# Linear attention with an ELU feature map on one core: three input buffers each instead of six, and a TensorE loop of three heads in nine turns

## The chip, the core and the metric

The kernel runs on one core of one Trainium2 chip. The metric is the device time of one execution in microseconds (us), median over the runs. Everything is bfloat16 in and out, with sums in fp32.

## What is computed

```python
B, H, S, D = 1, 32, 2048, 128
phi_q = where(q > 0, q + 1, exp(q)) + 1e-6
phi_k = where(k > 0, k + 1, exp(k)) + 1e-6
kv  = einsum("bhsd,bhse->bhde", phi_k, v)
z   = einsum("bhsd->bhd", phi_k)
num = einsum("bhqd,bhde->bhqe", phi_q, kv)
den = einsum("bhqd,bhd->bhq", phi_q, z)[..., None] + 1e-6
out = num / den
```

There are 32 independent heads. Each head reads q, k and v (512 KB each) and writes out (512 KB): 4 transfers of 512 KB a head, 128 in all.

## The kernel before, in words

A head's 2048 rows lie as 16 tiles of 128 x 128, 16 rows to a partition. The map phi(x) is formed as max(x, 0) + (min(exp(x), 1) + 1e-6). For a head h the steps are:

- **Loads** (L310 to L324): SyncE (SP) issues k, q and v into `k_sb`, `q_sb`, `v_sb`, each with `NBI` buffers (L189), head h in buffer h % NBI. Only v of head 0 has a buffer and a queue of its own (`v0_sb`, issued by ScalarE, L315).
- **k's map**: ScalarE forms exp(k) (`ek_sb`, L328), GpSimd max(k, 0) (`rk_sb`, L330), VectorE min(exp(k), 1) + 1e-6 (`emk_sb`, L334), and GpSimd adds the two for five of the sixteen tiles (L339). Both L328 and L330 read k's buffer.
- **kv and z**: TensorE multiplies phi(k)'s tiles with v into `kvz_ps` (L355, with one more column for z, L358), ScalarE and VectorE copy it out (L363, L365).
- **q's map**: TensorE transposes the 16 tiles of q into `x_ps` (L373), ScalarE, VectorE form exp, max and min from there (L384, L387, L390, L393).
- **Output**: TensorE multiplies phi(q) with kv into five banks `o_ps` (L411, L417), VectorE divides into `o_sb` (ten buffers, L432 and L438), and SP stores the head (L472).

**The order on each engine** is not the order of the text. A planner (`Plan`, L20) gets every step with a key, sorts each engine's steps by it (L54) and places a semaphore wait wherever a step reads or overwrites what another engine made. Keys are in heads. The keys of SP's queue matter here:

```python
load("k", k_sb, kf, h - NBI - (1.0 if h < 3 else 1.95))
load("v", v_sb, vf, h - NBI - 0.8)
load("q", q_sb, qf, h - NBI - 0.9)
late = h + 1.0 + 0.18 * h      # key of the store of head h
```

A load of head h waits until buffer h % NBI is free, that is, until the steps of head h - NBI that read it are done. SP works strictly in order: a load that waits holds up whatever stands behind it. The store's key grows by 1.18 a head and the load's by 1, so the stores fall back behind the loads in the queue as the kernel goes on; the last ten or so stores are issued after the last load.

**TensorE's program** has nine steps a head (two of transposes, two of kv, five output banks) after one step of warming up. It runs in three parts: some heads written out, then a hardware loop whose waits add a register to their constants, then the rest written out (`run`, L123). The loop begins at step 1 + LOOP * 9, has NBI * 9 steps and TURNS turns (L480): here 54 steps, or six heads, in four turns. L132 to L136 demand that the steps of all turns have the same waits and the same answer to whether the step raises a semaphore; a step raises one only where another engine needs it (`needed`).

Of the kernel before, what the change touches and what calls it, by code (L numbers as in the profile page):

```python
# [11 lines left out]
def _ap(base: bass.AP, elem_offset: int, dims):  # L12
    return bass.AP(base.tensor, base.offset + elem_offset, [list(base.ap[0])] + [list(d) for d in dims])
# [6 lines left out]
class Plan:  # L20
# [9 lines left out]
    def add(self, eng, key, emit, reads=(), writes=(), dma=None):  # L30
        op = Op()
        op.eng, op.key, op.emit, op.dma = eng, key, emit, dma
        op.deps, op.needed, op.clock = [], False, None
        op.reads, op.writes = tuple(reads), tuple(writes)
        for r in op.reads:
            w = self.writer.get(r)
            if w is not None:
                op.deps.append(w)
            if r[0].startswith("bank"):
                op.deps += [x for x in self.readers.get(r, []) if x.eng != eng]  # L40
        for r in op.writes:
            w = self.writer.get(r)
            if w is not None and (w.eng != eng or w.dma):
                op.deps.append(w)
            op.deps += [x for x in self.readers.get(r, []) if x.eng != eng or x.dma]
        for r in op.reads:
            self.readers.setdefault(r, []).append(op)
        for r in op.writes:
            self.writer[r] = op
            self.readers[r] = []  # L50
        self.ops.append(op)
        return op
# [7 lines left out]
    def emit(self, block, sems, dma_sem, loop):  # L60


        order = self.order()
        for op in self.ops:
            for d in op.deps:
                if not (d.eng == "pe" and op.eng == "pe"):
                    d.needed = True
        counts = {}
        for e, ops in order.items():
            n = 0  # L70
# [15 lines left out]
        while left:  # L86
            moved = False
            for e, ops in order.items():
                while at[e] < len(ops):
                    op = ops[at[e]]  # L90
# [85 lines left out]
def bass_standalone__linear_attn_elu__prompt_kernel(  # L176
# [9 lines left out]
    NH = B * H  # L186
    bf16 = mybir.dt.bfloat16
    fp32 = mybir.dt.float32
    NBI = 6  # L189
    NBO = 10  # L190
    NC = D + 1
    NB = 5
# [18 lines left out]

    PIECES = {NH - 2: ((0, 6), (6, NT)), NH - 1: ((0, 6), (6, 12), (12, NT))}
    EXTRA = {NH - 2: 0, NH - 1: 1}
    LOOP, TURNS = 3, 4

    qf = q.rearrange("b h s d -> (b h) s d")
    kf = k.rearrange("b h s d -> (b h) s d")
# [3 lines left out]
    with ExitStack() as es:  # L221
        def sb(name, shape, dt):
            return es.enter_context(nc.sbuf_tensor(name, shape, dt))

        k_sb = sb("k_sb", [P, NBI, NT * D], bf16)
        v_sb = sb("v_sb", [P, NBI, VW], bf16)
        q_sb = sb("q_sb", [P, NBI, NT * D], bf16)
        v0_sb = sb("v0_sb", [P, NT * D], bf16)
# [23 lines left out]

        for n, c in (("k", NBI), ("q", NBI), ("v", NBI), ("o", NBO + 3), ("x", 1)):
            for i in range(c):
# [17 lines left out]
        vfull = v_sb[:, :, :]  # L272
        pl.add("pool", -7, lambda g: g.memset(_ap(vfull, 0, [[VW, NBI], [GAP + GRP, 3], [1, GAP]]), 1.0), writes=[("vones",)])

# [31 lines left out]
        for h in range(NH):  # L306
            def at(name, key, h=h):
                return place.get((name, h), h + key)

            bi, b2, b3, bo = h % NBI, h % 2, h % 3, h % NBO  # L310

# [197 lines left out]
```

## Time and profile before

| | |
|---|---|
| median of 3 runs | 170.68 us (170.58 to 170.76) |
| the profiled execution's own time | 170.68 us |
| its span, first to last instruction | 168.8 us |
| TensorE's granted clock, mean | 0.994 |
| busy: PE / ACT / DVE / POOL | 158.0 / 157.3 / 149.6 / 105.5 us |
| moved by DMA | 67.31 MB, 399 GB/s over the span |

Outside the span lie 170.68 - 168.8 = 1.88 us. PE is TensorE's matmul, ACT ScalarE, DVE VectorE, POOL GpSimd, SP SyncE. The slices of the page are 168.8 / 40 = 4.22 us wide, a 9 in a row of slices means 90% or more. The DMA rows count packets on the core's 16 DMA engines; a transfer has landed when all 16 have marked it done.

### The profile page before, as it was taken

How to read it: one execution, taken by the hardware profiler on the slowest of the kernel's cores; microseconds unless marked ns; L12 is line 12 of the kernel's file. 1: busy time of each engine (PE TensorE's matmuls, PEld its weight loads, DVE VectorE, ACT ScalarE, POOL GpSimd, SP SyncE). 2: the span in 40 equal slices, each digit the busy share in tenths (PEclk: the TensorE clock that was granted, in tenths of full speed). 3: DMA queues.
4: the chain of work that ended last, by engine and by line, in shares of the span. 5: the costliest groups of instructions: out<-in, count | busy, mean ns of one | idle time of the engine just before them, and what ended most of it. 6: DMA issues, size and time to landing. Idle time of an engine off the chain costs nothing.

```text
span 168.8 us, 6570 instructions
## 1 busy us (share of the span) xinstructions
PE 158.0 (94%) x3089; PEld 151.7 (90%) x2401; DVE 149.6 (89%) x293; ACT 157.3 (93%) x180; POOL 105.5 (62%) x72
## 2 busy tenths in 40 slices
PE   7588999999999999999999999999999999999940
PEld 0488999999999999999999999999999999999830
DVE  0144999999999999999999999999999999999870
ACT  4599999999999999999999999999999999996960
POOL 3836866666677776666667776666667776666000
PEclk9999999999999999999999999999999999999997
DMA  5999999999999999999999999999999999999982
GB/s 204 412 414 411 412 406 409 406 415 408 411 414 409 415 416 415 418 413 419 415 414 415 416 413 420 413 419 415 413 416 418 417 414 415 411 413 415 412 333 104
DMA packets 22848, 67.31 MB, mean 399 GB/s; under 512 B 2097, under 2 KB 2609, under 8 KB 22833
## 3 DMA queue, kind: packets, MB, share of 16 engines
q1 hardware_dynamic: 22688, 66.59, 98.5%
q10 hardware_dynamic: 144, 0.52, 0.8%
q8 instruction: 9, 0.15, 0.3%
q14 instruction: 7, 0.05, 0.1%
HBM read 50.33 MB, written 16.78 MB: 398 GB/s over the span
## 4 chain that ended last, share of the span: by engine, by line
PE 87%; DMA 3%; DVE 3%; ACT 3%; issue 0%; SPq 0%
PE kvz_ps L355 36%; PE o_ps L411 32%; PE x_ps L373 16%; DMA q_sb<-in_q_dram 3%; DVE o_sb L438 1%; PE o_ps L277 1%; ACT eq_sb L384 1%; PE o_ps L417 1%; PE kvz_ps L277 1%; ACT ek_sb L328 1%; ACT rq_sb L387 1%; DVE emk_sb L334 0%; DVE rden_sb L460 0%; DVE den_sb L456 0%; SPq L320 0%
## 5 line engine op out<-in xcount | busy, mean ns | idle before, releaser
L384 ACT ACTIVATE eq_sb<-x_ps 128x1024 bf16<-128x1024 bf16 x64 | 72.4, 1349 | 3.4 <-PE x_ps L373 3.4
L339 POOL TENSOR_TENSOR rk_sb<-rk_sb,emk_sb 128x640 bf16<-128x640 bf16 x32 | 44.7, 1396 | 47.4 <-DVE emq_sb L393 41.2
L328 ACT ACTIVATE ek_sb<-k_sb 128x2048 bf16<-128x2048 bf16 x32 | 72.2, 2256 | 1.7 <-DMA k_sb<-in_k_dram 1.7
L438 DVE TENSOR_TENSOR o_sb<-o_ps,rden_sb 128x768 bf16<-128x768 f32 (+2 forms) x63 | 68.0, 1119 | 0.1
L355 PE MATMUL kvz_ps<-v_sb,rk_sb 128*128 128x128 bf16 (+1 forms) x512 | 67.6, 218 | 0.0
L330 POOL TENSOR_SCALAR rk_sb<-k_sb 128x2048 bf16<-128x2048 bf16 x32 | 60.6, 1892 | 2.7 <-DMA k_sb<-in_k_dram 2.0
L411 PE MATMUL o_ps<-kvs_sb,emq_sb 128*128 128x129 bf16 x474 | 60.6, 220 | 0.3 <-DVE o_sb L438 0.3
L411 PE MATMUL o_ps<-kvs_sb,rq_sb 128*128 128x129 bf16 x474 | 60.6, 220 | 0.0
L355 PE MATMUL kvz_ps<-v_sb,emk_sb 128*128 128x128 bf16 (+1 forms) x352 | 55.4, 219 | 1.2 <-DVE kvs_sb L365 1.2
L277 PE MATMUL kvz_ps<-ones_sb,rk_sb 128*128 128x1 bf16 x388 | 53.3, 166 | 0.0
L355 PEld LDWEIGHTS kvz_ps<-v_sb,rk_sb 128*128 128x128 bf16 x512 | 47.0, 97 | 1.5
L411 PEld LDWEIGHTS o_ps<-kvs_sb,rq_sb 128*128 128x128 bf16 x474 | 46.2, 97 | 0.0
L411 PEld LDWEIGHTS o_ps<-kvs_sb,emq_sb 128*128 128x128 bf16 x474 | 45.4, 97 | 0.6 <-DVE o_sb L438 0.4
L387 ACT ACTIVATE rq_sb<-x_ps 128x1024 bf16<-128x1024 bf16 x32 | 43.7, 1366 | 0.0
L277 PE MATMUL kvz_ps<-ones_sb,emk_sb 128*128 128x1 bf16 x228 | 37.8, 167 | 0.0
L373 PE MATMUL x_ps<-ident,q_sb 128*128 128x128 bf16 x512 | 34.6, 222 | 1.7 <-DMA q_sb<-in_q_dram 1.7
L373 PEld LDWEIGHTS x_ps<-ident,q_sb 128*128 128x128 bf16 x512 | 30.6, 99 | 5.6 <-DMA q_sb<-in_q_dram 5.6
L355 PEld LDWEIGHTS kvz_ps<-v_sb,emk_sb 128*128 128x128 bf16 x352 | 33.9, 97 | 1.5 <-issue 1.5
L334 DVE TENSOR_SCALAR emk_sb<-ek_sb 128x2048 bf16<-128x2048 bf16 x32 | 21.8, 682 | 8.8 <-ACT ek_sb L328 8.8
L390 DVE TENSOR_SCALAR rq_sb<-x_ps 128x1024 bf16<-128x1024 bf16 x32 | 21.8, 680 | 2.5 <-ACT eq_sb L384 2.5
L393 DVE TENSOR_SCALAR emq_sb<-eq_sb 128x2048 bf16<-128x2048 bf16 x32 | 22.1, 691 | 0.4 <-ACT eq_sb L384 0.4
L363 ACT ACTIVATE kvs_sb<-kvz_ps 128x128 bf16<-128x128 f32 x32 | 20.3, 634 | 0.0
(39 smaller groups left out, 78.2 us busy)
## 6 DMA issues: line engine op xcount, KB each, us to landing
k_sb<-in_k_dram SPq DMA_DIRECT2D x32, 512.0 KB, 13.2
q_sb<-in_q_dram SPq DMA_DIRECT2D x32, 512.0 KB, 13.2
v_sb<-in_v_dram SPq DMA_DIRECT2D x31, 512.0 KB, 13.6
out_dram<-o_sb SPq DMA_DIRECT2D x30, 512.0 KB, 13.8
out_dram<-o_sb SPq DMA_DIRECT2D x3, 192.0 KB, 4.7
v_sb<-in_v_dram ACTq DMA_DIRECT2D x1, 512.0 KB, 4.4
out_dram<-o_sb SPq DMA_DIRECT2D x1, 320.0 KB, 5.6
out_dram<-o_sb SPq DMA_DIRECT2D x1, 128.0 KB, 4.0
```

Source lines behind the costliest of these rows:

```text
L277: return pe.add_instruction(mybir.InstMatmult(name=nc.get_next_instruction_name(), engine=mybir.EngineType.PE, ldweights=False, ins=[pe.lo ...
L328: lambda a, bi=bi, b2=b2: a.activation(ek_sb[:, b2, :], k_sb[:, bi, :], ACT.Exp),
L330: pl.add("pool", h, lambda g, bi=bi, b3=b3: g.tensor_scalar(rk_sb[:, b3, :], k_sb[:, bi, :], BIG, 0.0, op0=ALU.min, op1=ALU.max), reads=[( ...
L334: lambda d, b2=b2, b3=b3: d.tensor_scalar(emk_sb[:, b3, :], ek_sb[:, b2, :], 1.0, EPS, op0=ALU.min, op1=ALU.add),
L339: pl.add("pool", h + 0.5, lambda g, added=added: g.tensor_tensor(out=added(rk_sb), in0=added(rk_sb), in1=added(emk_sb), op=ALU.add), reads ...
L355: last = pe.matmul(kvz_ps[:, 1 - l:NC + r], lhsT=w, rhs=rhs, start=first, stop=fin, skip_group_check=True)
L373: last = pe.transpose(xT_ps[:, j * P:(j + 1) * P], q_sb[:, bi, j * P:(j + 1) * P], ident[:])
L384: lambda a, b2=b2, c=cols(half): a.activation(eq_sb[:, b2, c], xT_ps[:, c], ACT.Exp),
L387: lambda a, b3=b3, c=cols(1): a.activation(rq_sb[:, b3, c], xT_ps[:, c], ACT.Relu),
L393: lambda d, b2=b2, b3=b3: d.tensor_scalar(emq_sb[:, b3, :], eq_sb[:, b2, :], 1.0, EPS, op0=ALU.min, op1=ALU.add),
L411: last = pe.matmul(o_ap, lhsT=x[:, b3, t * P:(t + 1) * P], rhs=kvs_sb[:, b3, :], start=first, stop=not first)
L438: return lambda d: d.tensor_tensor(out=o_sb[:, bo, t0:t1, :].rearrange("p (a b) d -> p a b d", b=n), in0=_ap(nfull(b), 512 * b + NC * (t0 ...
```

## The change

The number of buffers of k, q and v goes from six to three. The loop of TensorE's program follows it, since its size is NBI heads: 27 steps instead of 54, beginning at step 19 instead of 28, in nine turns instead of four. So 27 heads' worth of steps run in the loop where 24 did, and 8 heads' worth are written out in the program (2 before, 3 in the loop, 3 after) where 14 were (3, 6, 5). `Plan.emit` gets a passage that makes the answer of `needed` the same for a step in all turns: if one turn's step must raise its semaphore, those of all turns do.

```diff
@@ Plan.emit
+        eng, lo, size, turns = loop
+        for i in range(lo, lo + size):
+            turned = order[eng][i:lo + size * turns:size]
+            needed = any(op.needed for op in turned)
+            for op in turned:
+                op.needed = needed
@@ the kernel
-    NBI = 6
+    NBI = 3
     NBO = 10
@@
-    LOOP, TURNS = 3, 4
+    LOOP, TURNS = 2, 9
```

All keys that contain NBI move with it: the loads' keys become larger by 3, the stores' keys stay.

## The prediction

> **What bounds the kernel now.** I read the page's busy line first, then its slices, then the chain.
>
> ```profile
> PE 158.0 (94%) x3089; PEld 151.7 (90%) x2401; DVE 149.6 (89%) x293; ACT 157.3 (93%) x180; POOL 105.5 (62%) x72
> ...
> DMA  5999999999999999999999999999999999999982
> ...
> q8 instruction: 9, 0.15, 0.3%
> ...
> PE 87%; DMA 3%; DVE 3%; ACT 3%; issue 0%; SPq 0%
> ```
>
> Two resources are full at once. TensorE carries 87% of the chain; its timeline has the heads 4.73 us apart (kv of head 24 starts at 122.47, of head 30 at 150.86: 28.39 / 6) and no wait after 13.4 us. The DMA engines are full from the second slice to the 38th. Landing after landing, a transfer of 512 KB takes 1.27 us, so a head's four need 5.08 us, more than TensorE's 4.73. The stores' growing delay hides that: with 1 / 1.18 = 0.85 stores a head, 3.85 transfers need 4.89 us, still 0.16 too many. Loads therefore start with a lead and lose it. The next view is SP's: a load's time from issue to landing, over all of k.
>
> ```profile
> DMA to landing us min/median/max: 3.2/13.2/14.8
> ```
>
> The 3.2 is the first load, into an empty queue (1.27 of it data); 13.2 is ten transfers waiting ahead, not the memory being slow. The lead itself I take from the trace's landings beside the first instruction that reads the buffer: k of head 10 lands 7.1 us early, v of head 25 3.3, v of head 30 2.5. These are v of head 30's rows, SP's timeline and TensorE's:
>
> ```profile
> 134.87 0.55 SPq L320 DMA_DIRECT2D v_sb<-in_v_dram  x1
> ```
> ```profile
> DMA to landing us min/median/max: 13.5/13.5/13.5
> ```
> ```profile
> 150.86 0.22 PE L355 MATMUL kvz_ps<-v_sb,emk_sb 128*128 128x129 bf16 x1
> ```
>
> Issue 134.87 + 13.46 = 148.33 landed, 150.86 read: 2.5 us early. Last comes the end, in windows (DVE, ACT, PE busy; last two columns DMA share and GB/s):
>
> ```profile
> 162.00:164.00 2.00, 0.50 (x9) 0.33 (x6) 1.70 (x4) 1.68 (x6) 0.00 (x0) 1.00 0.86 337
> 164.00:166.00 2.00, 0.00 (x0) 0.00 (x0) 0.00 (x0) 0.00 (x0) 0.00 (x0) 1.00 0.68 253
> 166.00:168.80 2.80, 0.00 (x0) 0.00 (x0) 0.00 (x0) 0.00 (x0) 0.00 (x0) 0.66 0.06 24
> ```
>
> Compute is over at 164. The last store is issued at 164.38 and lands at 168.34. Of its 16 marks the first comes 1.74 us after the issue, the last 3.96: one DMA engine is 2.2 us behind the others and still works off older stores. That spread was 0.4 us until 17 us, jumps to 1.65 with the first block of TensorE code (q8, 16 KB, at 17.1 us, on one DMA engine) and grows to 4.6 by 164 us, about 0.13 per store from 90 us on. So the slowest DMA engine's total work sets the end, with compute 1.6 to 2 us ahead of it.
>
> **The change, part by part.** *Issue times.* Load h now waits for head h-3. k is released last (ScalarE's L328 and GpSimd's L330), so its load heads each burst on SP, and q, v and a store queue behind that wait. Does the queue run dry? For head 8, L330 of head 5 ends at 30.51; plus 0.1 to issue and 3.2 the earliest landing is 33.8. Before, k of head 8 landed at 33.69, and after, one to two stores go ahead of it (store 0 before k of head 6, store 1 before v of head 6): 33.69 + 2 x 1.27 = 36.2. The DMA side is later, so no gap. The tightest is head 5: free at 17.30, earliest 20.6; its DMA slot was 21.99 on the slowest engine and 20.34 on the first: at most 0.2 us of idling, not on the slowest. Later the distance grows (L330 of head 28 ends at 139.31, earliest 142.6, slot of head 31's k about 150). DMA stays full: 0 to +0.2 us.
>
> *Order of loads and stores.* At one time three heads fewer are in flight, so more stores stand ahead of each load. By the keys: v of head 30 had key 23.2 with stores 0 to 18 ahead, now 26.2 with 0 to 21: three more. The same count gives three more for v of 24, 25, 29, k of 31, q of 30 and 31; two for heads 20, 26, 27, 28. A store costs 1.27 us early and 1.36 to 1.44 in the landings around 145 us, so three late ones cost 4.15. Leads become: k of 10: 7.1 - 3.8 = 3.3; k of 20: 4.9 - 2.6 = 2.3; v of 24: 3.7 - 4.1 = -0.4; v of 25: 3.3 - 4.1 = -0.8; v of 28: 2.0 - 2.75 = -0.75; v of 29: 2.9 - 4.1 = -1.2; k of 31: 3.0 - 4.15 = -1.15; v of 30: 2.5 - 4.15 = -1.6; v of 31: 3.35 - 4.2 = -0.9. TensorE's first DMA wait thus falls on head 24 or 25, and the delays don't add: the largest, 1.6 us, is the shift of all that follows.
>
> *The end.* Compute ends 1.6 us later, the last store is issued at 164.38 + 1.6 = 166.0. First marks 1.74 later: 167.8. The slowest engine has the same stores and loads as before and, never having idled, reaches this store as before: 168.34. So the end moves by 0 to +0.3 us; the shift eats the distance between compute and the slowest engine. I take +0.2. The bounds: a slot early that idles by 0.2, a shift of 2.4 instead of 1.6 (+0.5); below, an engine that is spared code (rival).
>
> *The loop.* Eight jumps back instead of three, and 27 heads with register waits instead of 24. Before, a jump lies between bank 0 and bank 1 of heads 8, 14 and 20: there the matmuls start 55 to 58 ns apart, as in the heads without a jump, and head distances stay 4.73 to 4.75. Eight jumps: 0, at most 0.02 each or 0.2. This is hidden by nothing but TensorE's queue being ahead; a TensorE that waits for a load loses nothing by it either. Code: q8 blocks come at 17.1, 24.0, 31.5, 37.9, 45.3, 51.6, then at 142.4, 149.4, 156.7, so none within turns 2 to 4. One per 6.9 us is one per 1.45 heads; with 8 heads written out instead of 14, three to four of nine fall away, some 0.06 MB or 0.15 us of DMA over all engines.
>
> [...]
>
> *Rest.* The equal `needed` adds an increment to kv of head 29, whose first step no later load or GpSimd step needs: 0. The memset of v's ones (L273) halves from 0.58 us, while GpSimd waits 2.0 us for k behind it: 0. At the start SP blocks at k of head 3 until 5.93, with q and v of head 2 behind it; these land at 14.3 and 15.7 in DMA order either way: 0.
>
> **The rivals.** *A: a short queue runs the DMA slower.* Place: heads 5 to 31, where some four to seven transfers wait instead of ten. If a transfer takes 1% more (1.283), 128 of them add 1.6 us to the slowest engine, and loads reach TensorE late from head 20 on: 172.3. For it: the slots of heads 5 to 8 are near 3.2 us after issue, and the leads leave no room. Against: the first loads, with few in flight, also came 1.27 apart. It decides from 1.275 a transfer on.
>
> *B: less code, a slowest engine less behind.* A code block put its engine 1.26 us back. If the engine that ends last got one of the blocks that fall away (37.9 to 51.6), it ends 1.26 earlier, loads come as much earlier, the shift is 0.3: 170.68 - 1.26 = 169.4. Against: the last engine was already last after the blocks of 17.1 to 31.5, which stay.
>
> *C: each jump stalls.* A block takes 1.0 us on its engine and nothing lands under 3.2 us: five more jumps cost 5 to 16 us, 176 and up. Against: three jumps without a trace. [...]
>
> *D: nothing moves.* If landings slip less than the leads (say 2 us), no wait appears, and the time stays at 170.7.
>
> **How the numbers follow.** A measurement here can tell about 0.2%, 0.34 us, from no change: the edges are 170.34 and 171.02. The forecast (+0.2, 170.9; own range 170.5 to 171.6) has 0.43: 0.22 within the edges, 0.17 slower, since its bounds lean that way, 0.04 faster. A has 0.25, slower. B 0.20, faster. C 0.04, slower. D 0.08, the same. Faster 0.24, same 0.30, slower 0.46. From 169.4 (B in full) to 172.6 (A with 1.2% a transfer) leaves out C, the outer part of A and a little of B, under 0.2.
>
> **What the profile after would show.** Right: k's median from issue to landing near 6 to 8 us, no longer 13; DMA slices still full from the second on; new waits "PE L355 or L373 <- DMA" or "ACT L328 <- DMA" of 1 to 2 us in all, none before head 20; compute over near 165.6, last landing near 168.4; five or six q8 packets; no gap at bank 0 to bank 1 of heads 4, 7, 10 and so on. Wrong: DMA slices under 9 early, a head distance over 4.73 before head 20 (A), packets of q8 throughout (C), or a spread of the last marks well under 4 us (B).

## The result and the profile after

The changed kernel takes 172.59 us (median of 6 runs, 172.12 to 173.03), the kernel before 170.69 beside it (6 runs, 170.49 to 170.78): ratio 1.0112, 95% interval 1.0092 to 1.0133. It is slower by 1.9 us, where 170.9 was forecast: 0.01 us inside the upper edge of the widest range given (169.4 to 172.6), and outside the forecast's own (170.5 to 171.6). The profiled execution took 172.82 us, its span 171.0, against 170.68 and 168.8: +2.14 us. Times and ranges here and below leave out one execution (174.55 us, of the kernel with the waits alone) that lay over 1.5% above the fastest of its kernel.

From the page of the changed kernel, the rows that answer to those shown of before, and the row of GB/s by slice (40 slices of 4.28 us):

```profile
PE 158.4 (93%) x3089; PEld 150.4 (88%) x2401; DVE 150.1 (88%) x293; ACT 159.1 (93%) x180; POOL 105.2 (62%) x72
DMA  5999999999999999999999999999999999999964
GB/s 209 408 411 401 403 375 378 382 415 414 413 417 412 404 416 409 411 415 413 414 410 414 414 407 414 411 418 415 415 413 408 417 413 414 416 413 420 367 259 153
q8 instruction: 5, 0.08, 0.2%
DVE 41%; PE 32%; DMA 17%; ACT 5%; issue 2%; POOL 2%; SPq 0%
```

The same row of the kernel before:

```profile
GB/s 204 412 414 411 412 406 409 406 415 408 411 414 409 415 416 415 418 413 419 415 414 415 416 413 420 413 419 415 413 416 418 417 414 415 411 413 415 412 333 104
```

The engines work about as long as before (TensorE 158.4 us against 158.0; ScalarE, the most, 159.1 against 157.3) and the DMA row has 9s from the second slice to the 38th in both. But in slices 6 to 8 (21 to 34 us) DMA engines that count as full move 375 to 382 GB/s where they moved 406 to 409. The DMA view of the window from 20 to 31 us, before first and after second, says it in one row each:

```profile
DMA packets 1611, 4.52 MB, mean 411 GB/s; under 512 B 133, under 2 KB 133, under 8 KB 1610
```
```profile
DMA packets 1389, 4.11 MB, mean 374 GB/s; under 512 B 128, under 2 KB 128, under 8 KB 1388
```

Their queue rows give 102.9% and 99.9% of the engines' time to packets: engines that count as full, and packets that take longer (4 KB packets 173.1 ns in the mean instead of 161.0, 2 KB packets 89.7 instead of 84.1). The long middle, 45 to 140 us, shows a smaller loss of the same kind, again before and after:

```profile
DMA packets 13345, 39.45 MB, mean 415 GB/s; under 512 B 1205, under 2 KB 1205, under 8 KB 13339
```
```profile
DMA packets 13248, 39.20 MB, mean 413 GB/s; under 512 B 1196, under 2 KB 1196, under 8 KB 13243
```

0.25 MB less at 0.415 MB a us is 0.6 us in this stretch. Counted in the trace's packets of 45 to 140 us, 97.5% of the 4 KB packets of before took under 160 ns, and 83.1% of after; of the 2 KB packets 99.6% took under 85 ns, and 77.2%. From the landing of k of head 10 to that of k of head 30 lie 77 transfers of 512 KB: 1.272 us each before, 1.290 after. A landing is the last of 16 marks. Counted by the first of them the pace goes from 1.257 to 1.266 us. So half of the slowdown, 0.7 of 1.4 us, shows in the first marks too; the rest is the slowest engine falling further behind (last mark 2.0 us behind the first at k of head 10, 3.9 at k of head 30; before 2.1 and 3.3).

What that does to TensorE stands in the chain of waits (start, duration, what), here two pieces of it:

```profile
107.92 11.53 DMA v_sb<-in_v_dram
119.45 0.23 issue
119.67 0.34 PE kvz_ps L361 x3
```
```profile
137.77 11.59 DMA v_sb<-in_v_dram
149.36 0.23 issue
149.59 0.34 PE kvz_ps L361 x3
```

v of heads 23 and 29 lands 0.23 us before its first matmul: TensorE now waits for landings, and 17% of the chain is DMA, where it was 3%. (How the rest of the chain is split between DVE and PE differs from one execution of this kernel to the next; a second profile has DMA at 17% again, PE at 62%.) I count the shift in ScalarE's copies of kv (`kvs_sb`, one a head). These three lines of its timeline are heads 18, 19 and 20:

```profile
97.05 0.28 ACT L369 ACTIVATE kvs_sb<-kvz_ps 128x128 bf16<-128x128 f32 x1
102.42 0.28 ACT L369 ACTIVATE kvs_sb<-kvz_ps 128x128 bf16<-128x128 f32 x1 [0.23 <-PE kvz_ps L283]
107.44 0.30 ACT L369 ACTIVATE kvs_sb<-kvz_ps 128x128 bf16<-128x128 f32 x1
```

Head 19 comes 5.37 us after head 18, where 4.73 is a head's own time. Against before, head 17 is 0.4 us late, head 20 1.4, head 26 2.9, head 31 3.74. The last store is issued at 168.12 instead of 164.38, 3.74 later too, and the table of DMA issues gives its time to landing:

```profile
out_dram<-o_sb SPq DMA_DIRECT2D x1, 128.0 KB, 2.4
```

2.4 us instead of 3.96, with the 16 marks from 1.78 to 2.40 us after the issue where they came from 1.74 to 3.97: by now the slowest DMA engine has caught up, and compute sets the end. 3.74 - 1.57 = 2.17 us, against 2.14 measured.

### The profile page after: what moved, and what is told of

Same layout as the page of the kernel before. It is cut to its first block, busy times and chain, and to the rows that moved or that the text cites. A ratio compares the mean times of both kernels' runs of the same rounds, so it can differ in the third digit from the quotient of the medians.

```text
span 171.0 us, 6592 instructions
## 1 busy us (share of the span) xinstructions
PE 158.4 (93%) x3089; PEld 150.4 (88%) x2401; DVE 150.1 (88%) x293; ACT 159.1 (93%) x180; POOL 105.2 (62%) x72
## 4 chain that ended last, share of the span: by engine, by line
DVE 41%; PE 32%; DMA 17%; ACT 5%; issue 2%; POOL 2%; SPq 0%
DVE o_sb L444 18%; PE kvz_ps L361 14%; DMA v_sb<-in_v_dram 14%; PE o_ps L417 12%; DVE emk_sb L340 5%; DVE emq_sb L399 5%; DVE rq_sb L396 5%; PE x_ps L379 4%; DMA q_sb<-in_q_dram 3%; DVE o_sb L438 3%; ACT eq_sb L390 2%; DVE rden_sb L466 2%; POOL rk_sb L345 2%; DVE den_sb L462 2%; DVE kvs_sb L371 1%
## 5 line engine op out<-in xcount | busy, mean ns | idle before, releaser
L390 ACT ACTIVATE eq_sb<-x_ps 128x1024 bf16<-128x1024 bf16 x64 | 62.7, 1043 | 4.9 <-PE x_ps L379 4.9
L334 ACT ACTIVATE ek_sb<-k_sb 128x2048 bf16<-128x2048 bf16 x32 | 62.4, 1951 | 1.8 <-DMA k_sb<-in_k_dram 1.8
L417 PE MATMUL o_ps<-kvs_sb,emq_sb 128*128 128x129 bf16 x474 | 60.8, 220 | 0.7 <-issue 0.3
L417 PE MATMUL o_ps<-kvs_sb,rq_sb 128*128 128x129 bf16 x474 | 60.8, 220 | 0.0
L417 PEld LDWEIGHTS o_ps<-kvs_sb,emq_sb 128*128 128x128 bf16 x474 | 45.4, 97 | 1.3 <-issue 0.7
L417 PEld LDWEIGHTS o_ps<-kvs_sb,rq_sb 128*128 128x128 bf16 x474 | 46.2, 97 | 0.0
L361 PEld LDWEIGHTS kvz_ps<-v_sb,emk_sb 128*128 128x128 bf16 x352 | 33.3, 96 | 5.6 <-issue 4.1
L379 PE MATMUL x_ps<-ident,q_sb 128*128 128x128 bf16 x512 | 33.9, 219 | 1.8 <-DMA q_sb<-in_q_dram 1.8
L379 PEld LDWEIGHTS x_ps<-ident,q_sb 128*128 128x128 bf16 x512 | 29.8, 98 | 5.8 <-DMA q_sb<-in_q_dram 5.7
L393 ACT ACTIVATE rq_sb<-x_ps 128x1024 bf16<-128x1024 bf16 x32 | 33.8, 1055 | 0.0
L399 DVE TENSOR_SCALAR emq_sb<-eq_sb 128x2048 bf16<-128x2048 bf16 x32 | 22.7, 708 | 0.4 <-ACT eq_sb L390 0.4
L369 ACT ACTIVATE kvs_sb<-kvz_ps 128x128 bf16<-128x128 f32 x32 | 10.2, 319 | 0.5 <-PE kvz_ps L283 0.2
```

What stands on the lines that cost most here:

```text
L334: lambda a, bi=bi, b2=b2: a.activation(ek_sb[:, b2, :], k_sb[:, bi, :], ACT.Exp),
L361: last = pe.matmul(kvz_ps[:, 1 - l:NC + r], lhsT=w, rhs=rhs, start=first, stop=fin, skip_group_check=True)
L379: last = pe.transpose(xT_ps[:, j * P:(j + 1) * P], q_sb[:, bi, j * P:(j + 1) * P], ident[:])
L390: lambda a, b2=b2, c=cols(half): a.activation(eq_sb[:, b2, c], xT_ps[:, c], ACT.Exp),
L393: lambda a, b3=b3, c=cols(1): a.activation(rq_sb[:, b3, c], xT_ps[:, c], ACT.Relu),
L399: lambda d, b2=b2, b3=b3: d.tensor_scalar(emq_sb[:, b3, :], eq_sb[:, b2, :], 1.0, EPS, op0=ALU.min, op1=ALU.add),
```

## The experiments

Theories at the start: the slow transfers come from the short queue (rival A), from the order alone, or from the code's loop. When the runs had left none of these for the middle of the kernel, a fourth was formed: the new buffer count moves tensors in SBUF to other start addresses. Times are medians; ratios are to the kernel before, run beside it, with 95% intervals.

**The loop.** Three buffers, but TensorE's loop of six heads in four turns, as before.

```diff
-    LOOP, TURNS = 2, 9
+    LOOP, TURNS = 3, 4
-        ... ("pe", 1 + LOOP * 9, NBI * 9, TURNS)
+        ... ("pe", 1 + LOOP * 9, 2 * NBI * 9, TURNS)
```

> Three buffers as in the changed kernel, but TensorE's loop as before: 54 steps from step 28 in four turns. Theory Q (fewer transfers waiting make the DMA engines slower: 1.290 us a transfer between k of heads 10 and 30 instead of 1.272, and slow packets at 21 to 31 us) and theory O (three more stores stand ahead of each load): no change against the changed kernel, 172.1 to 173.0. Theory L (turns, jumps, code of the three-head loop): back to 170.4 to 171.0.

Measured: 173.14 us, ratio 1.0161 (1.0123 to 1.0199), nine q8 packets as before, 1.289 us a transfer. The loss is all there without the nine turns, so rival C falls and the loop costs nothing that shows in the time. Rival B falls too: four q8 packets fewer bring no time, and at k of head 30 the last mark is as far behind the first with five of them as with nine (3.9 and 3.8 us).

**A deep queue for k alone.** Six buffers for k, three for q and v. k blocks SP longest (71.6 us in 26 waits for GpSimd's max, in the changed kernel), so the queue ahead of its waits fills again.

```diff
+    NBK = 6
-        k_sb = sb("k_sb", [P, NBI, NT * D], bf16)
+        k_sb = sb("k_sb", [P, NBK, NT * D], bf16)
```
(and k's buffer index h % NBK; the loads' keys stay)

> The changed kernel with six buffers for k alone, keys and loop unchanged, so that a load of k no longer waits for GpSimd and its burst starts 1.5 to 3 us earlier, when q's and v's buffers are free. Theory Q: the queue is longer by that much (issue to landing of k 9 to 11 us instead of 7.8), and the loss shrinks: 171.3 to 172.1. Theories O and L: 172.3 to 172.9, as the order and the loop are the same.

Measured: 172.34 us, 1.0099 (1.0082 to 1.0116). Its issue row for k and its packets from 45 to 140 us:

```profile
k_sb<-in_k_dram SPq DMA_DIRECT2D x32, 512.0 KB, 12.1
```
```profile
DMA packets 13301, 39.23 MB, mean 413 GB/s; under 512 B 1197, under 2 KB 1197, under 8 KB 13297
```

The queue is nearly as deep as before (12.1 us against 13.2) and slices 6 to 8 are back at 399 to 404 GB/s, but a transfer still takes 1.289 us. So the slow middle does not come from a short queue. The time is above the 171.3 to 172.1 that the short queue would have given.

**The order alone.** The kernel before, its loads keyed as with three buffers.

```diff
-            load("v", v_sb, vf, h - NBI - 0.8)
+            load("v", v_sb, vf, h - 3 - 0.8)
```
(k and q alike)

> The kernel before, six buffers and its loop, but with the loads' keys of the changed kernel (h - 3 - ...), so that the stores stand among the loads as in the changed kernel. Theory O: the order alone makes the loss, 172.2 to 172.9. Theory Q: the buffers no longer hold the loads, the queue fills to some 10 to 13 us by head 10, leads fall by three stores (to -1.6 us at head 30) as forecast: 170.5 to 171.2.

Measured: 171.31 us, 1.0051 (1.0025 to 1.0077): +0.6 by the medians, +0.4 to +1.3 by the interval. A transfer takes 1.272 us, as before. TensorE's first longer head is head 19, and head 31 comes 2.15 us late, near the 1.6 of the forecast. The order is a part of the loss; 2.15 of the 3.74 us by which head 31 is late come with it alone.

**Stores later by three heads.** The changed kernel, with the stores put back behind the loads as they stood.

```diff
-            late = h + 1.0 + 0.18 * h
+            late = h + 4.0 + 0.18 * h
```

> The changed kernel with the stores' keys larger by 3 (h + 4.0 + 0.18 h), so that they stand among the loads as in the kernel before. Loads get their leads back (k of head 10 some 6 us early), but from head 5 to 8 only three transfers a head are there for 4.73 us, so DMA idles 0.9 us a head, some 2.8 us in all, that the slowest engine can't make up. Theory O: no TensorE wait on DMA, yet the end moves by that idling: 172.5 to 173.8. Theory Q: slow packets on top, 173.8 to 175. If DMA's total were not what sets the end: 170.7.

Measured: 175.23 us, 1.0258 (1.0241 to 1.0275), slower than any of the expectations. The page's slices of 26 to 39 us move 320, 313 and 322 GB/s. With three buffers, loads can't run ahead of the heads: three loads of 0.524 MB in a head of 4.67 us are 337 GB/s. Without early stores among them the DMA engines get less than the 406 to 415 GB/s that they move in these slices of the kernel before, and the stores have to be made up for later (a span of 173.3 us instead of 168.8). The busy share hardly tells, as the view of 26 to 39 us shows:

```profile
DMA packets 1476, 4.14 MB, mean 318 GB/s; under 512 B 127, under 2 KB 127, under 8 KB 1475
q1 hardware_dynamic: 1475, 4.12, 92.3%
```

That is 130 ns a packet (0.923 x 16 x 13 us / 1475), where the kernel before has 112 from 20 to 31 us (1.029 x 16 x 11 us / 1610). So a high busy share and long packets at a low rate came here with too few transfers on their way. The earlier stores that come with three buffers are needed there.

**The waits alone.** The order as in the run before last, and each load made to wait for the head three back, with six buffers.

```diff
-   ... writes=[(name, bi)], dma=(name, bi))
+   ... writes=[(name, bi), (name + "w", h % 3)], dma=(name, bi))
```
(and the readers of k, v and q in the fitting `reads`)

> Six buffers in memory, stores ordered and loads keyed as in the changed kernel (as e3), and every load made to wait for the steps that it waits for with three buffers (k for exp and max of head h - 3, q for the transposes, v for kv of h - 3), by naming three slots beside the six. Theory W (the waits and the bursts of issues that they make slow the DMA): pace between heads 10 and 30 back to 1.287 to 1.292 us a transfer and 172.3 to 173.0. Theory M (where the three buffers lie in memory slows the DMA's writes): 1.270 to 1.275 as in e3, and 171.1 to 171.7.

Measured: 172.03 us (171.41 to 173.10 over 6 runs), 1.0084 (1.0058 to 1.0110), between the two theories. The slices of 17 to 34 us fall to 377 to 387 GB/s, and from 45 us on the packets are as quick as before (97.5% under 160 ns); a transfer takes 1.258 us, less than either theory gave. Order and waits together do bring slow packets early; the slow middle needs something else, and what is left is where the buffers lie or how much memory they take. Against the order alone the intervals overlap, so the waits' own price is not settled.

**The room of six buffers, three of them used.**

```diff
-        k_sb = sb("k_sb", [P, NBI, NT * D], bf16)
+        k_sb = sb("k_sb", [P, 2 * NBI, NT * D], bf16)
```
(v and q alike)

> The changed kernel, three buffers in use, but k_sb, q_sb and v_sb allocated at six buffers' size, so that every tensor begins at the address that it has in the kernel before. Theory W: no change, 172.2 to 173.0 and 1.287 to 1.292 us a transfer. Theory M: if the other tensors' addresses do it, 1.272 and some 171.2 to 171.8; if it is the fewer addresses that the DMA writes to, no change.

Measured: 171.61 us, 1.0078 (1.0048 to 1.0109). The same instructions in the same order, the tensors at the addresses of before, and the middle moves its bytes again:

```profile
DMA packets 13385, 39.49 MB, mean 416 GB/s; under 512 B 1204, under 2 KB 1204, under 8 KB 13381
```

The pace came out only in part as expected (1.272): by the first mark it is 1.258 us, as before, but by the last still 1.287, since the slowest engine falls from 1.5 to 3.8 us behind the first here. The addresses of before don't take that away.

**k in three buffers, q and v in six.**

```diff
+    NBK = 3
-        k_sb = sb("k_sb", [P, NBI, NT * D], bf16)
+        k_sb = sb("k_sb", [P, NBK, NT * D], bf16)
```
(NBI stays 6; the loads keyed as with three)

> Order of stores as in the changed kernel, three buffers for k, six for q and v, TensorE's loop of six heads. k's load waits for GpSimd and heads each burst, as in the changed kernel. Theory W: bursts return, 1.285 to 1.292 a transfer, 172.2 to 173.0. Theory M, with e2 (k six, no gain): q and v are what counts, so 1.270 to 1.275 and 171.2 to 171.8.

Measured: 172.60 us (171.75 to 173.30), 1.0123 (1.0098 to 1.0147). The middle's packets are quick (97.5%), but slice 6 falls to 324 GB/s. By its time it is no faster than the changed kernel, though its start addresses modulo 512 are those of before and its pace (1.280 us) lies between. Its four runs spread over 1.5 us; that its early stretch costs what the middle gives back is a guess.

**The changed kernel once more,** unaltered, beside the runs on addresses.

> The changed kernel once more, for a second profile of it. All theories: 172.1 to 173.1. If the slow packets between 21 and 31 us come with the order of the first stores or the short queue, they come again, within 2 us of the same places and some 10 us of packet time in all; if they were chance, they are gone and the time is near 172.1.

Measured: 173.03 us (172.32 to 173.66), 1.0120 (1.0098 to 1.0142); 84.9% of the 4 KB packets under 160 ns. The middle repeats; the early slices are 348 to 380 GB/s here.

**64 bytes ahead of q.** A buffer of v has 4288 bytes a partition, so three of them are 12864, an odd multiple of 64, and `q_sb` and what follows lands on another remainder. Modulo 512, `q_sb` starts at 256 before and at 192 after, `o_sb` at 32 and 480; `k_sb` and `v_sb` keep 128.

```diff
+        sb("pad_q", [P, 32], bf16)
         q_sb = sb("q_sb", [P, NBI, NT * D], bf16)
```

> The changed kernel with an unused tensor of 64 bytes a partition ahead of q_sb. With three buffers of v (4288 bytes each) q_sb and the nine tensors up to kvs_sb begin at 192 bytes past a multiple of 512, with six at 256, and o_sb at 480 instead of 32; the 64 bytes put all back. Theory A (start addresses make one packet in six longer): 97% of the 4 KB packets at 159 ns again instead of 83%, pace 1.258 us a transfer on the first DMA engine and 171.5 to 172.1. Theory N (amount of memory, not its place): no change, 172.5 to 173.1 and 83%.

Measured: 171.76 us (171.29 to 172.94), 1.0074 (1.0048 to 1.0100); 97.6% under 160 ns.

```profile
DMA packets 13362, 39.49 MB, mean 416 GB/s; under 512 B 1202, under 2 KB 1202, under 8 KB 13358
```

64 unused bytes give back the 0.29 MB of the middle, and head 31 is 2.2 us late instead of 3.74 (in an execution of 171.29 us, the fastest of the six). In the middle the first head that takes longer than 4.75 us is head 24, where the forecast had it. That is not the address's doing: with `q_sb` at 256 too, the run with the room of six buffers has head 18 first, and the next run, with `q_sb` at 192, has head 24.

**64 bytes ahead of `o_sb` alone.**

```diff
+        sb("pad_o", [P, 32], bf16)
         o_sb = sb("o_sb", [P, NBO, NT, D], bf16)
```

> The changed kernel with the 64 unused bytes ahead of o_sb instead, so that only the stores' source comes back to 32 past a multiple of 512, and q_sb and the engines' tensors stay at 192. If the stores' reads of SBUF are what is longer: 97% at 159 ns and 171.5 to 172.1. If it is the place of q_sb or of the engines' operands: 83% and 172.4 to 173.1.

Measured: 173.32 us, 1.0133 (1.0109 to 1.0157), 83.4% under 160 ns, no better than the changed kernel and 0.2 us above what was expected. The stores' source is not it.

**The kernel before, moved.** 448 bytes ahead of q put `q_sb` at 192 (and what follows at the remainders of after), with nothing else changed.

```diff
+        sb("pad_q", [P, 224], bf16)
         q_sb = sb("q_sb", [P, NBI, NT * D], bf16)
```

> The kernel before with 448 unused bytes ahead of q_sb, so that q_sb and all behind it begin where they do in the changed kernel, modulo 512. Theory A: 83% at 159 ns and a pace 0.7% slower, which its slowest DMA engine adds up to 0.7 to 1.3 us: 171.3 to 172.0, with no change in order or waits. Theory N: 170.5 to 170.9.

Measured: 172.12 us (171.92 to 172.67), 1.0091 (1.0072 to 1.0110): +1.5 us, a little over the expected, with six buffers, the old order and the old loop. Its packets of 45 to 140 us and its last store (4.0 us to landing before):

```profile
DMA packets 13253, 39.25 MB, mean 413 GB/s; under 512 B 1195, under 2 KB 1195, under 8 KB 13247
```
```profile
out_dram<-o_sb SPq DMA_DIRECT2D x1, 128.0 KB, 5.5
```

Its heads stand where they stood (kv of head 31 copied at 158.41, before 158.66): TensorE's lead covers the slower loads, and the slowest DMA engine carries the loss to the end: the last store takes 5.5 - 4.0 = 1.5 us longer to land. Here the forecast's account of the end holds, with a term that it lacked.

**The kernel before, everything at a multiple of 512.** `k_sb`, `v_sb`, `q_sb` and `o_sb` start there, and the gaps between v's runs grow from 64 to 256 bytes.

```diff
-    GAP, GRP = 32, 8 * D
+    GAP, GRP = 128, 8 * D
+        sb("pad_k", [P, 192], bf16)     # ahead of k_sb
+        sb("pad_o", [P, 112], bf16)     # ahead of o_sb
```

> The kernel before with k_sb, v_sb, q_sb and o_sb each beginning at a multiple of 512, and v's gaps widened from 64 to 256 bytes so that v's runs begin at multiples of 256. If starts at such multiples save time on a packet beyond 159 and 84 ns: 169.5 to 170.4. If those are the floor already: 170.5 to 170.9.

Measured: 169.86 us (169.47 to 170.25), 0.9950 (0.9932 to 0.9968): faster than both kernels. 99.1% of the 4 KB packets take under 160 ns, and the last store lands 3.1 us after its issue instead of 4.0. Which of the moved tensors or gaps brings it is not separated.

```profile
out_dram<-o_sb SPq DMA_DIRECT2D x1, 128.0 KB, 3.1
```

**q moved back, or the engines' tensors moved back.** Two kernels that split the 64 bytes' effect: one moves `v0_sb` and the engines' tensors to their old remainders and leaves q at 192, the other moves q to 256 and leaves those.

```diff
 # first kernel
         q_sb = sb("q_sb", [P, NBI, NT * D], bf16)
+        sb("pad_v0", [P, 32], bf16)
 # second kernel
+        sb("pad_q", [P, 32], bf16)
         q_sb = sb("q_sb", [P, NBI, NT * D], bf16)
+        sb("pad_v0", [P, 224], bf16)
```

> The changed kernel with 64 unused bytes behind q_sb: q_sb, which DMA writes, stays at 192 past a multiple of 512, and the tensors behind it, which the engines write and read (ek_sb to kvs_sb), are back at 256. If DMA's own writes to q_sb are what is longer: 83% of the 4 KB packets at 159 ns and 172.4 to 173.2. If the engines' accesses at odd multiples of 64 bytes are what holds DMA's writes up: 97% and 171.4 to 172.1.

> The reverse: 64 unused bytes ahead of q_sb and 448 behind it, so that q_sb is back at 256 and the engines' tensors stay at 192. If DMA's own writes count: 97% at 159 ns and 171.4 to 172.1. If the engines' accesses count: 83% and 172.4 to 173.2.

Measured: the first 172.66 us, 1.0113 (1.0092 to 1.0134), 84.7% under 160 ns; the second 172.13 us (171.24 to 173.12), 1.0097 (1.0064 to 1.0130), 97.5%. Their packets of 45 to 140 us, in this order:

```profile
DMA packets 13278, 39.25 MB, mean 413 GB/s; under 512 B 1195, under 2 KB 1195, under 8 KB 13273
```
```profile
DMA packets 13375, 39.49 MB, mean 416 GB/s; under 512 B 1203, under 2 KB 1203, under 8 KB 13371
```

By the packets it is q's own start address. By the time the second is not told from the changed kernel alone; its slices 6 to 8 move 367 to 390 GB/s, and its runs spread over 1.9 us. Taken together, the four kernels of three buffers and the loop of three heads with q at 192 (1.0112, 1.0120, 1.0133, 1.0113) average 1.0120, the three with q at 256 (1.0078, 1.0074, 1.0097) 1.0083: 0.37% or 0.6 us, some 0.3 to either side by their intervals. With the other runs of that order and those waits taken in (1.0161 and 1.0099 at 192, 1.0084 and 1.0123 at 256) it is 1.0123 against 1.0091, 0.3% or 0.5 us.

**The changed kernel, everything at a multiple of 512.**

```diff
-    GAP, GRP = 32, 8 * D
+    GAP, GRP = 128, 8 * D
+        sb("pad_k", [P, 192], bf16)     # ahead of k_sb
+        sb("pad_q", [P, 128], bf16)     # ahead of q_sb
+        sb("pad_o", [P, 112], bf16)     # ahead of o_sb
```

> The changed kernel with the addresses of e12: k_sb, v_sb, q_sb, the engines' tensors and o_sb at multiples of 512, v's gaps 256 bytes. If order and queue cost with three buffers what e9 shows (1.1 us) and the alignment gives what e12 shows (-0.8): 170.7 to 171.3. If the three buffers eat what the alignment gives: 171.5 to 172.

Measured: 170.43 us (169.60 to 171.44, 10 runs), 0.9988 (0.9961 to 1.0014), a little under the 170.7 to 171.3 that was expected, 99.1% under 160 ns; slice 6 moves 323 GB/s. With the addresses at multiples of 512, three buffers run like the kernel before; beside the kernel before with its own at multiples of 512 (169.86) the change still costs about 0.6 us. So the same alignment is worth 2.1 us with three buffers (172.59 to 170.43) and 0.8 with six.

## Why the prediction was wrong, point by point

- **Issue times: "DMA stays full: 0 to +0.2 us". This step failed.** The DMA row stays at 9, as said, but engines that count as full moved less. The forecast took the pace of before, 1.27 us a transfer, as given for the changed kernel, and put a slower one into a rival alone; it measured 1.290. With 77 transfers at +0.018 that is 1.4 us of lateness between head 10 and head 30. About half of it goes with q's start address (the first mark's pace, 1.266 against 1.257 to 1.260 where q is moved back); the rest is the slowest engine falling further behind, which it also does with the addresses of before (1.287). The low rate before that (20 to 31 us, 4.11 MB instead of 4.52) is another part: k of head 10 landed at 47.42, 0.9 later than worked out, and at 47.24 with the order alone.
- **Rival A had the price and not the mechanism, which is luck.** It gave 1.283 us a transfer and 172.3 us, and its sign, a head distance over 4.73 before head 20, came too. But with a deep queue and the new addresses the transfer stays at 1.289, and with a short queue and the old addresses the middle's packets are as quick as before. What makes the middle's packets longer is that `q_sb` starts 192 bytes past a multiple of 512 instead of 256 (83 to 85% of the 4 KB packets under 160 ns, against 97.5% where it alone is moved back). The prediction saw in the buffer count a matter of waits and order, and not that it also moves every tensor behind.
- **Order: three more stores ahead of a late load. Right in kind.** k's median from issue to landing is 7.8 us (6 to 8 forecast). The leads became 2.3 us for k of head 10 (3.3 forecast) and 0.1 to 0.2 for v of 25 and 30, which is none: TensorE waits. Head 6 takes 4.82 us instead of 4.67, but beside a jump of the loop (below); the waits that last begin at head 18 instead of 24 (at head 19 with the order alone), and v of head 30 landed at 154.50 instead of 152.5. With the order alone head 31 is 2.15 us late (1.6 forecast, bound 2.4), and the time +0.6 instead of +0.2.
- **The end: right as an account, with the wrong shift put in.** "The shift eats the distance between compute and the slowest engine" is what happened: 3.74 of shift less 1.57 of distance. A shift larger than the distance goes over to compute, and the last store lands 2.4 us after its issue. With 1.6 put in, it gave +0.2.
- **The loop: right in the time, and at seven of the eight jumps.** The branch that ends a turn takes 0.21 to 0.23 us on TensorE's sequencer at the eight jumps, and beside seven of them the matmuls go on starting at most 58 ns apart. Beside the first (head 4, 34.8 us) two starts come 293 and 518 ns after the ones before them, which the view of waits has as `PEld o_ps L417 <- issue: 0.7, 2, 0.5`, and head 6 takes its 4.82 us. What TensorE waited for there is not shown. With four turns of six heads head 6 takes 4.67 us, and no time is gained (173.14 us). With 64 bytes ahead of `o_sb` it takes 6.33 us in the same loop of three heads, with k in six buffers 4.66. Rival C's price, at least 1.0 us for each jump, shows at none of the eight of the changed kernel's profile. Five q8 packets came where five or six were expected, and none from 32.2 to 109.6 us.
- **SP's waits: right.** The burst of a head hangs on GpSimd's max, 26 times in the view of SP's waits:

```profile
SPq L122 <- POOL rk_sb L336: 71.6, 26, 3.3
```

- **D, nothing moves,** fell with the waits at head 18.

The +1.9 us in parts, as the runs bear them out: q's start address about 0.5 to 0.6 on three buffers (1.5 on the kernel before alone, where nothing else is late); the order of the stores about 0.6 (0.4 to 1.3); the rest, some 0.7, is not traced to one cause. With everything at multiples of 512 in both kernels the change costs 0.6 us, as much as the order alone, so this rest goes when all start addresses are at multiples of 512 and v's gaps are widened with them; whether it is theirs, or only finds more room there, no run tells. The slow stretch of 17 to 34 us is a candidate: with k in six buffers, where slices 6 to 8 are back at 399 to 404 GB/s, the time is 0.2% under the average of the four kernels with q at 192, within the intervals. Against it, the aligned kernel of three buffers has one of the slowest slices of all (323) and still loses no more. The parts share the same lead and don't add strictly.

**Open.** Why packets slow down between 17 and 34 us: the changed kernel and all others with early stores and waits like three buffers' have it, in depths that differ from run to run (slice 6 from 323 to 394 GB/s), and the order alone has it at 25 to 34 us (378); the kernel before and its two moved versions do not. It goes with a queue that has run down: at 20 us ten transfers were issued and not landed in the kernel before, four in the changed kernel and in the order alone, whose median to landing (13.0 us) hides it. But with k in six buffers it is four as well, and that run shows only a trace of it. Open too is why v's 2 KB packets lengthen when q moves (82.8% under 85 ns in the kernel before with q moved, against 99.6%), though `v_sb` stays where it was.

## What to carry to other kernels

A buffer count is also a layout: here it moved `q_sb` from 256 to 192 modulo 512, and 64 bytes of padding took the time from 172.59 to 171.76 us. When the last tensors of a list shift, compare the start addresses of DMA destinations before and after, and try padding before believing a story of waits. A DMA row full of 9s said here that packets were under way on the engines, not that they moved quickly (375 to 382 GB/s under 9s, where before had 406 to 409); read GB/s and the packet times beside it. And read the pace by the first mark (1.266 us) as well as by the last (1.290), since the last mixes in how far one engine has fallen behind. And where two resources run with little lead, price a slower transfer over the whole kernel: 1.4% on each of 77 was 1.4 us here.

## What the runs showed of the hardware

- **The start address of one DMA destination in SBUF, `q_sb`, is worth 0.9% of the kernel before, and some 0.3% with three buffers.** `q_sb` at 192 instead of 256 (modulo 512): the 4 KB packets under 160 ns fall from 97.5% to between 82 and 86%, their mean goes from 159.5 to between 160.1 and 160.6 ns, and the time of the kernel before rises by 1.5 us. All of k, v, q and o at multiples of 512, with v's gaps widened: 99.1%, and 0.8 us faster. Why is not shown. Not every start off a multiple of 256 goes with long packets: `k_sb` stands at 128 in the kernel before, where 97.5% are under 160 ns, and `o_sb` at 32 instead of 480 made no difference (83.4% against 83.1%). And only one packet in six takes longer in the changed kernel (16.9% take 160 ns or more), not each.
- **The drift of the slowest DMA engine went away in two of the kernels.** In the kernel before it falls further behind from 90 us on, 1.284 us a transfer up to 115 us and 1.289 from there to 145; with everything at multiples of 512 it keeps 1.258 to 1.259 from 45 to 145 us, and the last store lands 3.1 us after its issue instead of 4.0. Why the drift goes is not settled: it is also gone where six buffers' loads are ordered and wait as with three, at the old addresses (1.258).
- **Loads keyed three heads back widen the runs.** The kernel before spreads over 0.2 to 0.8 us in the five sets of its runs, and its two moved versions over 0.8; those with loads keyed three heads back spread over 0.5 to 1.9 us, but for k in six buffers (0.24).
